# Block 0 of a convolution and feed-forward kernel: fp32 operands in its first layer replaced by three passes of 12-bit parts, with the order of the start rewritten

## The chip, the cores and the metric

The kernel runs on one core of one Trainium2 chip. The metric is the device time of one execution in microseconds (us): the median of several runs. The engines are TensorE (PE: matmuls; PEld is its weight load), VectorE (DVE), ScalarE (ACT), GpSimd (POOL) and SyncE (SP, which here only issues DMAs).

## The reference

`x` is 8 x 4096 x 192 in fp32, `weight` 8 x 7, `w_in` 192 x 2048 and `w_out` 2048 x 192. The two large weights are given in 64-bit floating point.

```python
w = exp(weight - max(weight)); w = w / (sum(w) + 1e-9)   # per head, 7 taps
out = einsum('hk,bskhg->bshg', w, windows(x))            # causal convolution along the sequence, 24 channels a head
x = out.reshape(32768, 192)
h = x @ w_in
g = h * clip(h + 3, 0, 6) / 6
result = (g @ w_out).astype(float32)
```

## The kernel before

**Blocks.** The 32768 tokens are 32 blocks of 1024 (two halves of 512, one half in the lower 64 partitions, one in the upper). Of each block, `y` (the convolution; three thirds of 64 channels per half) is multiplied by `w_in` (first layer: 8 chunks `c` of 128 columns and two groups, OWN with `y` as it lies, OTHER with the halves' partitions swapped by DMA), the gate is applied on ACT (`relu`, L308) and DVE (`gate`, L312), and `g` is multiplied by `w_out` (second layer).

**Blocks 1 to 31** write each operand of the first layer as parts of 12 significant bits. The high part is x times 1 - 2^-13, rounded to the short format fp32r as it is written; the low part is x minus the high one. `PASSES` then takes three products for each fp32 one: high by high, low weights by high y, full weights by low y. A unit of `first_layer` (L508) is 3 passes x 3 thirds x 2 halves = 18 matmuls into two banks of PSUM (a slot), then one relu and one gate over both banks. `second_layer` (L593) is a Strassen scheme in fp32.

**Block 0** works in plain fp32. `half_mm` (L302) does one third of one half; a part `(c, group)` is 6 matmuls into two banks, taken from a list of eight, with two relus and two gates of 512. `out_direct` (L347) is its second layer, in fp32: three groups of 64 matmuls; a group goes through the eight chunks of `w_out` in order, eight matmuls a chunk.

**The start, by engine order.** Everything from `tc.manual_schedule()` on runs on each engine in the order of the code. While block 0 begins, 16 units of weights (8 of `w_in`, then 8 of `w_out`, 384 columns each) are rounded from 64 to 32 bits by the class `Rounding`:

- `load`: DMA from SP into a stage buffer; unit n + 4 is loaded at the join of unit n.
- `split` (L177, L181): two bit operations on DVE, `scale` and `top`.
- `clamp` (L189, L192, L195): three operations on ACT.
- `join` (L198, L202 on DVE, then the product L206 on POOL), which writes the weights.

`stg` has 8 stage buffers, `cnv` 4 sets of work tiles. Of the convolution of block 0, third 2 is made on PE (seven taps as diagonal matrices, L794), third 0 on DVE in half-width taps (L261), third 1 on ACT (tap 0), DVE (taps 1 to 4) and PE (taps 5, 6). `begin` starts parts with the thirds 2 and 0 while third 1 is under way. The loop over the 16 parts joins, clamps and splits a unit in ten of its turns (`slots`); units 13 to 15 follow behind the loop. `prepare`, inside `out_direct`, then cuts all of `w_in` into its three parts with `w_parts` (ACT L480 and L487, POOL L483), convolves block 1 (L899) and cuts its y.

Since the start is laid out by hand, the time depends on which engine stands where when a unit's weights, a third of y or a slot is due.

Of the kernel before, what the change touches and what calls it, by code (L numbers as in the profile page):

```python
# [8 lines left out]
ALU = mybir.AluOpType  # L9
# [22 lines left out]
def kernel(  # L32
# [39 lines left out]
    start_pools, first_in = ExitStack(), ExitStack()  # L72
    stg = start_pools.enter_context(tc.tile_pool(name="stg", bufs=8))
    cnv = start_pools.enter_context(tc.tile_pool(name="cnv", bufs=4))
    fi = first_in.enter_context(tc.tile_pool(name="fi", bufs=1, side="right"))
# [40 lines left out]
    zeros = cnv.tile([P, N], F32, name="zeros", bufs=1)  # L116
    nc.vector.memset(zeros[:], 0.0)


    w_in = fi.tile([P, NP, K3, P], F32, name="w_in")  # L120


# [10 lines left out]
    def stage():  # L133
        return stg.tile([P, WS, 2], U32, name="stage")

    def load_w_in(j):
        st = stage()
        for half in range(2):
            nc.sync.dma_start(  # L139
                out=st[half * D2 : (half + 1) * D2].rearrange("p (s f) w -> p s (f w)", s=K3),  # L140
                in_=w_in_bits[j + half * NP].rearrange("p s f w -> p s (f w)"),
            )
        return st

    def load_w_out(j):
        st = stage()
        nc.sync.dma_start(
            out=st[:].rearrange("p (k d) w -> p k (d w)", k=2), in_=w_out_bits[:, j]
        )
        return st  # L150
# [7 lines left out]
    class Rounding:  # L158
# [13 lines left out]
        def split(self):  # L172
# [4 lines left out]
            nc.vector.tensor_scalar(  # L177
# [3 lines left out]
            nc.vector.tensor_scalar(  # L181
# [15 lines left out]
        def join(self):  # L197
# [9 lines left out]
                out=self.dst, in0=self.sig[:], in1=self.scale[:].bitcast(F32), op=ALU.mult  # L207
            )
    def w_in_unit(j):
        return Rounding(lambda: load_w_in(j), w_in[:, j].rearrange("p s f -> p (s f)"))  # L210

    def w_out_unit(j):
        dst = w_out[:, j, B11 : B22 + 1].rearrange("p b d -> p (b d)")
        return Rounding(lambda: load_w_out(j), dst)
# [29 lines left out]
    y_swapped = fi.tile([P, K3, N], F32, name="y_swapped")  # L244
    OWN, OTHER = 0, K3
# [29 lines left out]
    def swap_first(part):  # L275
        swap(y_swapped[:, part], y[:, part])

    g = cst.tile([P, NP, 2, G, N], F32, name="g")
# [6 lines left out]
    free_banks = list(range(2 * 4))  # L285

    def take():
        return free_banks.pop(0)

    def give(b):  # L290
        free_banks.append(b)

    def half_mm(k, b, w, third_of_y, start=False, stop=False, onto=False):

        r = slice(k * D2, (k + 1) * D2)  # L300
        src = y[r, third_of_y] if third_of_y < K3 else y_swapped[r, third_of_y - K3]
        nc.tensor.matmul(  # L302
            out=psum[:, b], lhsT=w[r], rhs=src, start=start, stop=stop,
            skip_group_check=onto,
        )
# [9 lines left out]

    def h_mm(c, group, bs, s, order=range(K3)):

        for k in range(2):
            half_mm(k, bs[k], w_in[:, c, s], group + s, s == order[0], s == order[-1])

    def g_of(c, group, k):

        return g[:, c, k, k if group == OWN else 1 - k]

    def h_out(c, group, bs, between):
        for k, b in enumerate(bs):
            relu(g_of(c, group, k), psum[:, b])
        between()
        for k, b in enumerate(bs):
            gate(g_of(c, group, k), psum[:, b])  # L330
            give(b)

# [44 lines left out]
    def out_direct(i, work):  # L383

        parts = [(k, q) for k in range(G) for q in range(G * NQ)]
        for r in range(0, len(parts), 4):
            b = take()
# [16 lines left out]
            give(b)  # L404
# [20 lines left out]

    def product(bank, j, n, q, ks=every, **tokens):
        x, w = prod[n]
        return mm(bank, j, S3 if n == 7 else x, w, q, ks, True, True, **tokens)

    def four(*parts):  # L430

        b = take()
        bank = psum[:, b]
        side_by_side(*[product(bank, j, n, q) for j, (n, q) in enumerate(parts)])
        return b, bank

    def three(n, n4, q4):
        return four(*[(n, q) for q in range(NQ)], (n4, q4))

    def by_quarters(n, q):  # L440

        b = take()
        bank = psum[:, b]
        w = NP // 4
        side_by_side(
            *[product(bank, j, n, q, range(j * w, (j + 1) * w)) for j in range(4)]
        )
        return b, bank
# [27 lines left out]
    def r32(ap):  # L476
        return ap.bitcast(F32R)

# [6 lines left out]
    def w_parts(high, low, full, w):  # L485
        high_of(high, w)
        nc.scalar.copy(out=r32(full), in_=w)  # L487
        low_of(low, w, high, nc.gpsimd)

    free_slots = list(range(4))  # L490
    y_own, y_other, pools, s1 = [], [None], [], []

    def swap_parts():
        y_other[0] = pools[0].tile([P, 2, K3, N], F32, name="y_other", tag="other")
        for n in range(2):
            swap(y_other[0][:, n], y_own[n])


    def first_layer(i, jobs):

        def unit(n):
            group, c = divmod(n, NP)
            slot = free_slots.pop(0)
            for m_, (wn, yn) in enumerate(PASSES):
                for s in range(K3):
                    for k in range(2):
                        r = slice(k * D2, (k + 1) * D2)
                        nc.tensor.matmul(  # L508
                            out=psum[:, 2 * slot + k], lhsT=r32(w_in_parts[wn][r, c, s]),
                            rhs=r32(y_other[0][r, yn, s] if group else y_own[yn][r, s]),  # L510
                            start=m_ == s == 0, stop=m_ == 2 and s == K3 - 1,
                            skip_group_check=True,
                        )
            both = psum[:, 2 * slot : 2 * slot + 2]
            to = g4[:, c, 1:3] if group else g4[:, c, 0::3]
            relu(to, both)
            gate(to, both)
            free_slots.append(slot)
# [259 lines left out]

    with tc.manual_schedule():
# [10 lines left out]
        pe_taps = KC - 2  # L790
# [8 lines left out]
        b = take()  # L799
        for _ in range(3):  # L800

            nc.tensor.matmul(
                out=psum[:, b], lhsT=zeros[:, 0:P], rhs=zeros[:], start=True, stop=True
            )
        for k in range(KC):
# [3 lines left out]
        b1 = take()  # L809
        pe_tap(b1, 1, pe_taps, pe_taps)  # L810


        order = (pe_third, 0, 1)
        parts = [(c, group) for p in range(0, NP, 2) for group in (OWN, OTHER)
                 for c in (p, p + 1)]
        early = {}

        def begin(c, group):
            early[c, group] = take(), take()
            for s in order[:2]:  # L820
                h_mm(c, group, early[c, group], s, order)
# [3 lines left out]
        for k, u in enumerate(conv0[: per + 2 * pe_taps]):  # L825
            if k == 5:
                split(0)
                clamp(0)
            elif k == per - 3:
                join(0, more=False)  # L830
                split(1)
                nc.scalar.copy(out=y[:, pe_third], in_=psum[:, b])
                give(b)
                swap_first(thirds[pe_third])
                clamp(1)
            elif k in (per, per + 1):
                if k == per:
                    swap_first(thirds[0])
                    load(AHEAD)
                    begin(0, OWN)  # L840
                    pe_tap(b1, 1, pe_taps + 1, pe_taps)
                continue
            elif k == per + 4:
                join(1)
                split(2)
                clamp(2)
            u()
        add(y[:, 1], psum[:, b1], y[:, 1])
        give(b1)
        swap_first(thirds[1])  # L850
        join(2)
        split(3)
        clamp(3)
        split(4)

        for c, group in ((0, OTHER), (1, OWN), (1, OTHER)):
            begin(c, group)
        for c, group in parts[: len(early)]:
            h_mm(c, group, early[c, group], order[2], order)

        slots = [0, 1, 3, 4, 6, 7, 9, 10, 12, 13]
        n = 3
        for slot, (c, group) in enumerate(parts):
            first = slot < len(early)
            if first:
                bs = early[c, group]
            else:
                bs = take(), take()
                for s in range(K3):
                    h_mm(c, group, bs, s)  # L870
            more = slot in slots

            def between():
                if more:
                    join(n)
                    clamp(n + 1)

            if slot == 6:
                x_tiles[1] = load_x(1)
            h_out(c, group, bs, (lambda: None) if first else between)  # L880
            if more:
                split(n + 2)
                if first:
                    between()
# [109 lines left out]
```

## Time and profile before

| | us |
|---|---|
| median of 3 runs (2225.63 to 2225.75) | 2225.64 |
| the profiled execution | 2225.73 |
| its span | 2223.6 |
| busy: PE, DVE, ACT, POOL | 2216.4, 1810.3, 938.1, 819.8 |
| chain that ended last: L593, L508, L302, L347 | 49%, 46%, 2%, 2% |
| relu 128x512 (L308), 128x1024 | 0.68, 1.12 |
| clamp L189, L192, L195 | 0.62, 0.62, 0.57 |
| product on POOL L206 on w_in, on w_out | 1.08, 1.04 |

Durations are the means of one instruction. On ACT and DVE the next instruction may start some 0.05 to 0.1 us before the end of the one ahead of it, so the distance between starts is the better price. The granted clock of PE was 0.999. A timeline row is: start, duration, engine, line, operation, output <- input, shape, and how many like ones are merged; in brackets stands the idle time before it and what ended it.

### The profile page before, as it was taken

The page shows a single profiled execution, that of the slowest core. Times are in us where ns is not written, and L with a number is a line of the kernel's source. Part 1 is how long each engine was busy: PE and PEld are TensorE (multiplying, and loading weights), DVE is VectorE, ACT ScalarE, POOL GpSimd, SP SyncE. Part 2 cuts the span into 40 slices and gives each one's busy share as a digit, 9 for nine tenths or more (in the row PEclk, how much of TensorE's full clock was granted, in tenths as well). Part 3 has the DMA queues.
Part 4 walks back from the last instruction along what each step waited for, and adds up shares of the span by engine and source line. Part 5 has one row for each costly group of instructions (what it writes and reads, how often), then busy time and mean ns, then how long its engine had stood idle before and what let it go on. Part 6 is the DMA issues. An engine that isn't in the chain of part 4 may idle for free.

```text
span 2223.6 us, 49133 instructions
## 1 busy us (share of the span) xinstructions
PE 2216.4 (100%) x21496; PEld 1536.0 (69%) x21496; DVE 1810.3 (81%) x1607; ACT 938.1 (42%) x1182; POOL 819.8 (37%) x692
## 2 busy tenths in 40 slices
PE   9999999999999999999999999999999999999999
PEld 5467776677766777766777667776677776677766
DVE  8788888887888888888888888888888888788866
ACT  7444443344433444334444334443344433344433
POOL 2434432344422444223443224442244432344322
PEclk9999999999999999999999999999999999999999
DMA  6233223333234342243322333323433224333232
GB/s 157 58 68 72 49 44 77 70 70 65 38 67 77 63 77 35 57 77 70 70 52 43 75 73 67 70 36 64 77 65 75 39 53 77 70 70 55 40 60 34
DMA packets 248613, 142.10 MB, mean 64 GB/s; under 512 B 207024, under 2 KB 212144, under 8 KB 248400
## 3 DMA queue, kind: packets, MB, share of 16 engines
q1 hardware_dynamic: 229912, 105.08, 23.3%
q0 software_dynamic: 17248, 33.64, 8.7%
q8 instruction: 168, 2.75, 0.5%
q10 hardware_dynamic: 1240, 0.27, 0.1%
q14 instruction: 45, 0.37, 0.1%
HBM read 31.72 MB, written 25.17 MB: 26 GB/s over the span
## 4 chain that ended last, share of the span: by engine, by line
PE 99%; DMA 0%; DVE 0%; SPq 0%; ACT 0%; issue 0%; DVEq 0%; ACTq 0%
PE psum L593 49%; PE psum L508 46%; PE psum L302 2%; PE psum L347 2%; DMA x<-in_x_dram 0%; SPq L106 0%; SPq L139 0%; DVE top L181 0%; PE psum L794 0%; DVE y L261 0%; DVE results L462 0%; SPq L95 0%; ACT y L808 0%; ACT scale L192 0%; ACT sig L195 0%
## 5 line engine op out<-in xcount | busy, mean ns | idle before, releaser
L593 PE MATMUL psum<-g,w_out 128*32 128x512 f32 (+1 forms) x6712 | 967.4, 552 | 0.0
L308 ACT ACTIVATE g<-psum,half 128x1024 f32<-128x1024 f32 (+1 forms) x528 | 574.2, 1092 | 487.8 <-PE psum L508 459.8
L312 DVE SCALAR_TENSOR_TENSOR g<-g,psum 128x1024 f32<-128x1024 f32 (+1 forms) x528 | 619.6, 1185 | 195.5 <-ACT g L308 195.1
L556 POOL TENSOR_TENSOR s<-g 128x256 f32<-128x256 f32 x248 | 267.0, 1077 | 1252.9 <-DVE g L312 877.3
L593 PEld LDWEIGHTS psum<-g,w_out 128*32 128x32 f32 x6712 | 371.8, 110 | 246.3 <-issue 126.9
L508 PE MATMUL psum<-y,w_in 64*128 64x512 f32 x4464 | 515.3, 388 | 0.0
L508 PE MATMUL psum<-y_other,w_in 64*128 64x512 f32 x4464 | 510.9, 386 | 0.0
L508 PEld LDWEIGHTS psum<-y,w_in 64*128 64x128 f32 x4464 | 415.8, 184 | 112.3 <-issue 26.0
L508 PEld LDWEIGHTS psum<-y_other,w_in 64*128 64x128 f32 x4464 | 418.1, 184 | 87.8
L593 PE MATMUL psum<-s,w_out 128*32 128x512 f32 (+1 forms) x3272 | 465.4, 570 | 0.0
L899 DVE SCALAR_TENSOR_TENSOR y<-x,c_sb,y 128x1536 f32<-128x1536 f32 x186 | 336.7, 1810 | 8.4 <-ACT y L897 7.2
L418 POOL TENSOR_TENSOR s<-g 128x1024 f32<-128x1024 f32 x93 | 297.8, 3203 | 25.0 <-DVE g L312 25.0
L593 PE MATMUL psum<-g,w_s 128*32 128x256 f32 x1240 | 282.8, 379 | 0.0
L593 PEld LDWEIGHTS psum<-s,w_out 128*32 128x32 f32 x3272 | 154.5, 110 | 80.2 <-issue 48.3
L593 PEld LDWEIGHTS psum<-g,w_s 128*32 128x32 f32 x1240 | 136.4, 110 | 67.7
L418 DVE TENSOR_TENSOR s<-g 128x2048 f32<-128x2048 f32 (+1 forms) x93 | 177.2, 1933 | 1.1
L593 PE MATMUL psum<-s,w_s 128*32 128x256 f32 x744 | 170.7, 379 | 0.0
L556 DVE TENSOR_TENSOR g<-g 128x1024 f32<-128x1024 f32 x124 | 151.7, 1224 | 6.0 <-DVE g L556 0.9
L418 DVE TENSOR_TENSOR g<-g 128x2048 f32<-128x2048 f32 x62 | 139.1, 2284 | 0.0
L462 DVE TENSOR_TENSOR p<-psum,p 32x256 f32<-32x256 f32 (+1 forms) x93 | 47.7, 513 | 95.5 <-PE psum L593 94.1
L462 DVE TENSOR_TENSOR results<-psum,results 32x256 f32<-32x256 f32 (+3 forms) x128 | 69.3, 541 | 51.1 <-issue 47.6
L590 ACT COPY psum<-psum 32x512 f32<-32x512 f32 x93 | 51.3, 551 | 135.3 <-PE psum L593 135.3
(87 smaller groups left out, 1152.4 us busy)
## 6 DMA issues: line engine op xcount, KB each, us to landing
y_other<-y SPq DMA_DIRECT2D x124, 384.0 KB, 5.0
g<-g POOLq DMA_DIRECT2D x62, 512.0 KB, 5.0
out_dram<-results SPq DMA_DIRECT2D x378, 64.0 KB, 2.0
x<-in_x_dram SPq DMA_DIRECT2D x53, 388.5 KB, 7.0
stage<-in_moe_w_in_dram SPq DMA_DIRECT2D x16, 192.0 KB, 4.6
stage<-in_moe_w_out_dram SPq DMA_DIRECT2D x8, 384.0 KB, 7.3
x<-in_x_dram SPq DMA_DIRECT2D x7, 384.0 KB, 6.5
x<-in_x_dram POOLq DMA_DIRECT2D x2, 388.5 KB, 5.4
```

Source lines behind the costliest of these rows:

```text
L302: nc.tensor.matmul(out=psum[:, b], lhsT=w[r], rhs=src, start=start, stop=stop, skip_group_check=onto,)
L308: nc.scalar.activation(r6, h, ACT.Relu, bias=half[:], scale=1.0 / 6.0)
L312: nc.vector.scalar_tensor_tensor(out=g_, in0=g_, scalar=1.0, in1=h, op0=ALU.min, op1=ALU.mult)
L347: lambda p=p: nc.tensor.matmul(out=bank[j * QS : (j + 1) * QS, tokens], lhsT=w_out[:, p, w, cols], rhs=x[:, p, tokens], start=(first and p ...
L418: engine.tensor_tensor(out=o[:, r], in0=a[:, r], in1=b[:, r], op=op)
L462: nc.vector.tensor_tensor(out=out, in0=x, in1=y, op=op)
L508: nc.tensor.matmul(out=psum[:, 2 * slot + k], lhsT=r32(w_in_parts[wn][r, c, s]), rhs=r32(y_other[0][r, yn, s] if group else y_own[yn][r, s ...
L556: engine.tensor_tensor(out=o, in0=p, in1=q, op=op)
L590: streams[3].append((t - 0.5, lambda: fn(*args, **kw)))
L593: nc.tensor.matmul(out=out, lhsT=w, rhs=x, start=start, stop=True, tile_position=(0, j * QS), skip_group_check=True,)
L899: jobs.append(lambda k=k: nc.vector.scalar_tensor_tensor(out=y[:], in0=x[:, :, k : k + N], scalar=c_sb[:, k : k + 1], in1=y[:], op0=ALU.mu ...
```

## The change

Everything concerns the start and block 0.

- The three parts of `w_in` are made unit by unit in a new step `part`: the high part on ACT, the full one as a copy and the low one as a subtraction on POOL, from `sig`, into which the product now goes. `part(n)` stands half a step behind `join(n)`: with the second of two units of the first layer. `w_parts` leaves `prepare`.
- The first layer of block 0 uses the three passes (`products`), slots of two banks, and one relu and one gate of 1024 a unit. The thirds of y are cut into high (ACT) and low (DVE) one by one, and both are swapped: twelve swap DMAs instead of six.
- Taps 3 to 6 of third 1 are on PE instead of taps 5 and 6.
- A unit of weights is joined with every second unit of the first layer, so eight in the loop (units 2 to 9) and six behind it (10 to 15).
- The stages of `w_in` lie in the part of `g` that is written last; `stg` has 4 buffers (for `w_out` alone) and `cnv` 3.

```diff
+    g = cst.tile([P, NP, 2, G, N], F32, name="g")
+    zeros = g[:, 0, 0, 0]
+    w_in_parts = [cst.tile([P, NP, K3, P], F32, name=f"w_in{n}") for n in range(3)]
+    y_own = [cst.tile([P, K3, N], F32, name=f"y{n}") for n in range(2)]
+    y_other = cst.tile([P, 2, K3, N], F32, name="y_other")
...
+    early_stages = [
+        g[:, c].rearrange("p h k n -> p (h k n)").bitcast(U32)[:, t : t + 2 * WS]
+        .rearrange("p (f w) -> p f w", w=2)
+        for c in range(NP - 4, NP) for t in (0, 2 * WS)
+    ]
...
             nc.gpsimd.tensor_tensor(
-                out=self.dst, in0=self.sig[:], in1=self.scale[:].bitcast(F32), op=ALU.mult
-            )
+                out=self.sig[:] if len(self.dst) > 1 else self.dst[0],
+                in0=self.sig[:], in1=self.scale[:].bitcast(F32), op=ALU.mult,
+            )
+
+        def part(self):
+            if len(self.dst) > 1:
+                high, low, full = self.dst
+                nc.scalar.mul(r32(high), self.sig[:], CUT)
+                nc.gpsimd.tensor_copy(out=r32(full), in_=self.sig[:])
+                nc.gpsimd.tensor_tensor(
+                    out=r32(low), in0=self.sig[:], in1=high, op=ALU.subtract
+                )
...
+    def products(n, slot, s, steps=range(3), begin=False, end=False):
+        group, c = divmod(n, NP)
+        for m_ in steps:
+            wn, yn = PASSES[m_]
+            for k in range(2):
+                r = slice(k * D2, (k + 1) * D2)
+                nc.tensor.matmul(
+                    out=psum[:, 2 * slot + k], lhsT=r32(w_in_parts[wn][r, c, s]),
+                    rhs=r32(y_other[r, yn, s] if group else y_own[yn][r, s]),
+                    start=begin and m_ == 0, stop=end and m_ == 2, skip_group_check=True,
+                )
...
-        pe_taps = KC - 2
+        pe_taps = 3
...
+        for u in conv0[5 : per - 3]:
+            u()
+        join(0, more=False)
+        split(1)
+        high_y(pe_third, psum[:, b : b + 1])
+        part(0)
+        clamp(1)
+        for u in conv0[per - 3 : per]:
+            u()
+        low_y(pe_third, psum[:, b : b + 1])
+        high_y(0, all_of(0))
+        low_y(0, all_of(0))
+        load(AHEAD)
+        thirds_of(0, (pe_third, 0))
+        join(1)
+        split(2)
+        for u in conv0[per + 2 : per + 2 * pe_taps]:
+            u()
+        part(1)
         add(y[:, 1], psum[:, b1], y[:, 1])
-        give(b1)
-        swap_first(thirds[1])
-        join(2)
+        high_y(1, all_of(1))
+        low_y(1, all_of(1))
+        clamp(2)
         split(3)
-        clamp(3)
-        split(4)
...
+        thirds_of(1, (pe_third, 0))
+        thirds_of(0, (1,), True)
+        thirds_of(NP, (pe_third, 0))
+        thirds_of(1, (1,), True)
+        thirds_of(NP, (1,), True)
...
+        n = 2
+        for at, k in enumerate([0, 1, NP, NP + 1] + [
+            c + group * NP for c in range(2, NP) for group in range(2)
+        ]):
...
+            relu(to, both)
+            if at % 2:
+                part(n)
+                clamp(n + 1)
+            else:
+                join(n)
+            gate(to, both)
+            free_slots.append(slot)
+            if at % 2:
                 split(n + 2)
-                if first:
-                    between()
                 n += 1
...
         def prepare():
-            for n in range(0, NP, 4):
-                r = slice(n, n + 4)
-                w_parts(*[w[:, r] for w in w_in_parts], w_in[:, r])
             for job in conv_jobs(1):
                 job()
```

`high_y` and `low_y` cut one third of y; `low_y` also issues its swaps. `thirds_of` begins or continues a unit with the thirds named. Of the units, n = c is OWN and n = NP + c is OTHER, with NP = 8.

More of the change, by code (lines that the diff above doesn't have):

```diff
@@ L71 @@
     ps = ctx.enter_context(tc.tile_pool(name="ps", bufs=1, space=bass.MemoryType.PSUM))
[L72 to L75, printed above, removed]
+    start_pools = ExitStack()
+    stg = start_pools.enter_context(tc.tile_pool(name="stg", bufs=4))
+    cnv = start_pools.enter_context(tc.tile_pool(name="cnv", bufs=3))
     def x_source(i):
@@ L115 @@
     diag = cnv.tile([P, KC, P], F32, name="diag", bufs=1)
-    zeros = cnv.tile([P, N], F32, name="zeros", bufs=1)
-    nc.vector.memset(zeros[:], 0.0)
-    w_in = fi.tile([P, NP, K3, P], F32, name="w_in")
+    g = cst.tile([P, NP, 2, G, N], F32, name="g")
+    zeros = g[:, 0, 0, 0]
+    nc.vector.memset(zeros, 0.0)
+    w_in_parts = [cst.tile([P, NP, K3, P], F32, name=f"w_in{n}") for n in range(3)]
+    y_own = [cst.tile([P, K3, N], F32, name=f"y{n}") for n in range(2)]
+    y_other = cst.tile([P, 2, K3, N], F32, name="y_other")
     w_out = cst.tile([P, NP, 7, DH], F32, name="w_out")
@@ L131 @@
     assert 2 * D == WS
-    def stage():
-        return stg.tile([P, WS, 2], U32, name="stage")
+    early_stages = [
[3 more added lines that the diff above has]
+    ]
     def load_w_in(j):
-        st = stage()
+        st = early_stages[j]
         for half in range(2):
@@ L145, in load_w_out @@
     def load_w_out(j):
-        st = stage()
+        st = stg.tile([P, WS, 2], U32, name="stage")
         nc.sync.dma_start(
@@ L149, in load_w_out @@
         )
-        return st
+        return st[:]
     EXP1 = 1 << 20
@@ L170, in load, with split @@
             self.st = self.load_words()
-        def split(self):
+        def split(self, engine=nc.vector):
             high = self.st[:, :, 1]
@@ L176, in split @@
             self.sig = cnv.tile([P, WS], F32, name="sig")
-            nc.vector.tensor_scalar(
+            engine.tensor_scalar(
                 out=self.scale[:], in0=high, scalar1=0x7FF00000, scalar2=None,
@@ L180, in split @@
             )
-            nc.vector.tensor_scalar(
+            engine.tensor_scalar(
                 out=self.top[:], in0=high, scalar1=0xFFFFF, scalar2=0x100000,
@@ L206, in join, with r32 @@
             nc.gpsimd.tensor_tensor(
-                out=self.dst, in0=self.sig[:], in1=self.scale[:].bitcast(F32), op=ALU.mult
-            )
+                out=self.sig[:] if len(self.dst) > 1 else self.dst[0],
+                in0=self.sig[:], in1=self.scale[:].bitcast(F32), op=ALU.mult,
+            )
+        def part(self):
[6 more added lines that the diff above has]
+                )
+    def r32(ap):
+        return ap.bitcast(F32R)
     def w_in_unit(j):
-        return Rounding(lambda: load_w_in(j), w_in[:, j].rearrange("p s f -> p (s f)"))
+        dst = [w[:, j].rearrange("p s f -> p (s f)") for w in w_in_parts]
+        return Rounding(lambda: load_w_in(j), dst)
     def w_out_unit(j):
         dst = w_out[:, j, B11 : B22 + 1].rearrange("p b d -> p (b d)")
-        return Rounding(lambda: load_w_out(j), dst)
+        return Rounding(lambda: load_w_out(j), [dst])
     def w_sums(sums):
@@ L243 @@
     y = ys.tile([P, K3, N], F32, name="y")
-    y_swapped = fi.tile([P, K3, N], F32, name="y_swapped")
-    OWN, OTHER = 0, K3
+    OWN, OTHER = range(2)
     def conv_units(i, parts, cuts=1):
@@ L273, in swap @@
         nc.sync.dma_start(out=to[0:D2], in_=part[D2:P])
-    def swap_first(part):
-        swap(y_swapped[:, part], y[:, part])
-    g = cst.tile([P, NP, 2, G, N], F32, name="g")
     g4 = g[:].rearrange("p c h k n -> p c (h k) n")
@@ L284 @@
     psum = ps.tile([P, 2 * 4, N], F32, name="psum")
[L285 to L304, printed above, removed]
-        )
+    free_slots = list(range(4))
     def relu(r6, h):
@@ L314, in gate @@
         )
[L316 to L327, printed above, removed]
-        between()
-        for k, b in enumerate(bs):
-            gate(g_of(c, group, k), psum[:, b])
-            give(b)
     def dff_half(k):
@@ L386, in out_direct @@
         for r in range(0, len(parts), 4):
-            b = take()
+            b = 2 * free_slots[r // 4]
             bank = psum[:, b]
@@ L403, in out_direct @@
             nc.vector.transpose(out=xt[:], in_=bank)
-            give(b)
             for j, (k, q) in enumerate(parts[r : r + 4]):
@@ L424 @@
     }
[L426 to L448, printed above, removed]
     def rows(q):
@@ L472 @@
     m = slice(0, DH)
-    def r32(ap):
-        return ap.bitcast(F32R)
     def high_of(out, x):
@@ L483, in low_of, with swap_parts, places @@
         engine.tensor_tensor(out=r32(out), in0=x, in1=high, op=ALU.subtract)
[L485 to L494, printed above, removed]
-        for n in range(2):
-            swap(y_other[0][:, n], y_own[n])
+    s1 = []
+    def swap_parts(thirds=slice(0, K3)):
+        for n in range(2):
+            swap(y_other[:, n, thirds], y_own[n][:, thirds])
+    def products(n, slot, s, steps=range(3), begin=False, end=False):
[9 more added lines that the diff above has]
+                )
+    def places(n, slot):
+        group, c = divmod(n, NP)
+        return g4[:, c, 1:3] if group else g4[:, c, 0::3], psum[:, 2 * slot : 2 * slot + 2]
     def first_layer(i, jobs):
         def unit(n):
-            group, c = divmod(n, NP)
             slot = free_slots.pop(0)
-            for m_, (wn, yn) in enumerate(PASSES):
+            for m_ in range(3):
                 for s in range(K3):
[L506 to L515, printed above, removed]
+                    products(n, slot, s, (m_,), s == 0, s == K3 - 1)
+            to, both = places(n, slot)
             relu(to, both)
@@ L777, in join, with part @@
             load(n + AHEAD)
+    def part(n):
+        units[n].part()
     with tc.manual_schedule():
@@ L797, in pe_tap @@
             )
-        b = take()
+        b, b1 = (2 * free_slots[-1] + k for k in range(2))
         for _ in range(3):
             nc.tensor.matmul(
-                out=psum[:, b], lhsT=zeros[:, 0:P], rhs=zeros[:], start=True, stop=True
+                out=psum[:, b], lhsT=zeros[:, 0:P], rhs=zeros, start=True, stop=True
             )
@@ L808 @@
         nc.scalar.mul(y[:, 1], x0[:, 1, 0:N], c_sb[:, 0:1])
[L809 to L815, printed above, removed]
-        early = {}
[L818 to L821, printed above, removed]
+        for k in range(pe_taps, KC):
+            pe_tap(b1, 1, k, pe_taps)
@@ new lines, with thirds_of, high_y, low_y @@
+        early = {}
+        def thirds_of(n, which, end=False):
+            if n not in early:
+                early[n] = free_slots.pop(0)
+            for s in which:
+                products(n, early[n], s, begin=s == pe_third, end=end)
+        def high_y(s, of):
+            high_of(y_own[HIGH][:, thirds[s]], of)
+        def low_y(s, of):
+            low_of(y_own[LOW][:, thirds[s]], of, y_own[HIGH][:, thirds[s]], nc.vector)
+            swap_parts(thirds[s])
+        def all_of(s):
+            return y[:, thirds[s]]
@@ L823 @@
         conv0 = conv_units(0, thirds[:pe_third], 2)
         per = len(conv0) // pe_third
[L825 to L846, printed above, removed]
-            u()
+        for u in conv0[:5]:
+            u()
@@ new lines @@
+        split(0)
+        clamp(0)
+        for u in conv0[5 : per - 3]:
[16 more added lines that the diff above has]
+            u()
@@ L848 @@
+        part(1)
         add(y[:, 1], psum[:, b1], y[:, 1])
-        give(b1)
-        swap_first(thirds[1])
-        join(2)
+        high_y(1, all_of(1))
+        low_y(1, all_of(1))
+        clamp(2)
         split(3)
-        clamp(3)
-        split(4)
[L856 to L861, printed above, removed]
@@ L862 @@
-        n = 3
-        for slot, (c, group) in enumerate(parts):
-            first = slot < len(early)
-            if first:
-                bs = early[c, group]
-            else:
[L868 to L881, printed above, removed]
+        thirds_of(1, (pe_third, 0))
@@ new lines @@
+        thirds_of(0, (1,), True)
[6 more added lines that the diff above has]
+        ]):
+            if at == 6:
+                x_tiles[1] = load_x(1)
+            if k in early:
+                slot = early[k]
+            else:
+                slot = free_slots.pop(0)
+                for m_ in range(3):
+                    for s in range(K3):
+                        products(k, slot, s, (m_,), s == 0, s == K3 - 1)
+            to, both = places(k, slot)
+            relu(to, both)
[7 more added lines that the diff above has]
+            if at % 2:
@@ L882 @@
                 split(n + 2)
-                if first:
-                    between()
                 n += 1
@@ L891 @@
         start_pools.close()
-        late = ctx.enter_context(tc.tile_pool(name="late", bufs=1, reuse_waits="tile"))
-        w_in_parts = [late.tile([P, NP, K3, P], F32, name=f"w_in{n}") for n in range(3)]
         def conv_jobs(i):
@@ L915, in prepare @@
         def prepare():
-            for n in range(0, NP, 4):
-                r = slice(n, n + 4)
-                w_parts(*[w[:, r] for w in w_in_parts], w_in[:, r])
             for job in conv_jobs(1):
                 job()
-            first_in.close()
-            later = ctx.enter_context(tc.tile_pool(name="later", bufs=1, reuse_waits="tile"))
-            y_own.extend(later.tile([P, K3, N], F32, name=f"y{n}") for n in range(2))
-            pools.append(ctx.enter_context(tc.tile_pool(name="oth", bufs=1, reuse_waits="tile")))
             x_tiles[2] = load_x(2, nc.gpsimd)
```

## The prediction

> **What bounds the kernel now.** The page says PE 100% busy, which says little, so I first read the chain of waits in order of time.
>
> ```profile
> 17.28 41.27 PE psum L302 x184
> 58.56 41.34 PE psum L347 x384
> 99.89 32.87 PE psum L508 x288
> ```
>
> Block 0's first layer (L302), its second (L347) and block 1's first layer (L508) follow each other without a gap. From 99.89 us on, 31 equal blocks of 32.87 + 35.47 us follow, which the change leaves alone: its worth is the shift of 99.89. L302 and L508 do the same work: 48 and 144 pairs of half products, 41.27 us for 46 pairs (0.90 each) against 32.87 (0.228 each). Operands of 12 bits are the cheaper: 16 units of 9 x 0.228 = 2.05 us, where 16 units now take 16 x 3 x 0.86 = 41.3. If PE were all, 8.4 us would go.
>
> Next the busy times in stretches of 10 us (columns: stretch, sum, PE, PEld, DVE, ACT, POOL, clock, DMA share, GB/s):
>
> ```profile
> 24.00:34.00 10.00, 10.00 (x47) 6.02 (x46) 8.82 (x20) 9.81 (x18) 2.01 (x2) 1.00 1.02 266
> 34.00:44.00 10.00, 10.00 (x47) 6.73 (x45) 10.00 (x20) 9.81 (x19) 4.19 (x4) 1.00 0.70 208
> 44.00:54.00 10.00, 10.00 (x48) 6.70 (x46) 9.71 (x22) 9.84 (x19) 2.17 (x4) 1.00 0.00 0
> ```
>
> ACT and DVE are as full as PE. ACT's timeline shows that it has no air in it:
>
> ```profile
> 42.19 0.61 ACT L189 ACTIVATE sig<-scale,bias_e 128x384 f32<-128x384 uint32 x1
> 42.84 0.61 ACT L192 ACTIVATE scale<-sig,bias_e 128x384 uint32<-128x384 f32 x1
> 43.48 0.57 ACT L195 ACTIVATE sig<-stage 128x384 f32<-128x384 uint32 x1
> 43.97 2.39 ACT L308 ACTIVATE g<-psum,half 128x512 f32<-128x512 f32 x4
> 46.24 0.61 ACT L189 ACTIVATE sig<-scale,bias_e 128x384 f32<-128x384 uint32 x1
> ```
>
> One clamp takes 1.78 us (42.19 to 43.97; the last of its three only 0.49), four relus 2.27 (0.57 each). Block 0 has 16 clamps and 32 relus. The last look is at DVE and POOL behind the layer:
>
> ```profile
> 60.95 0.55 DVE L198 SCALAR_TENSOR_TENSOR scale<-stage,scale 128x384 uint32<-128x384 uint32 x1
> ...
> 61.89 0.35 DVE L177 TENSOR_SCALAR scale<-stage 128x384 uint32<-128x384 uint32 x1
> 62.04 1.06 POOL L206 TENSOR_TENSOR w_out<-sig,scale 128x384 f32<-128x384 f32 x1 [4.46 <-DVE sig L202]
> 62.16 1.16 DVE L181 TENSOR_SCALAR top<-stage 128x384 uint32<-128x384 uint32 x1
> ...
> 63.24 0.55 DVE L198 SCALAR_TENSOR_TENSOR scale<-stage,scale 128x384 uint32<-128x384 uint32 x1
> ...
> 66.09 1.01 POOL L206 TENSOR_TENSOR w_out<-sig,scale 128x384 f32<-128x384 f32 x1 [0.50 <-DVE sig L202]
> ```
>
> L181 takes 0.35 elsewhere; started during POOL's product it takes 1.16 and ends with it. So a unit with a split goes round in 2.29 us (60.95 to 63.24), and from the join of unit 13 (60.95) to the end of the product of unit 15 (67.10) it is 6.15. The eight L347 matmuls on unit 15 (its chunk is the last of eight in group 0) begin 7 x 1.72 us after 58.56, at 70.6 (1.72 = 8 x 41.34 / 192). Unit 15 has 3.5 us to spare. That is the number the change uses up.
>
> **The change, step by step.** My sum is a time for unit 15's product, since only that chunk lets PE go on.
>
> *Until clamp 2.* Up to 12.7 us nothing moves. Then POOL has three operations a w_in unit instead of one. The copy has no row: one input of 128 elements took 0.29 (AFFINE_SELECT), two inputs 0.46 where DVE leaves it alone (L565) and 1.0 at 384 elements, so I scale 0.29 by 1.0 / 0.46 to 0.63; the ends are 0.29 and 1.08 (the mean of L206 on w_in). The subtraction is put at 1.0, as L206 of that shape. By the L181 row DVE's taps (0.41 each) and POOL's operations exclude each other, so I let them alternate. Top of unit 1 ends at 13.86; three taps, a copy and a subtraction 16.4; low of third 2 (0.65) and of third 0 (0.6) 17.7; join 1 (0.95) 18.65; split 2 (0.55) 19.2; POOL's product until 19.95; four taps, copy and subtraction 23.05; the sum with PE's taps (0.6) 23.65; the high part of third 1 on ACT (0.6) 24.25; clamp 2 behind it, 26.0. Without any exclusion it is 23.8. In this time ACT stands at two new waits with clamp 2 queued behind them: the high part of unit 1's weights waits for POOL's product (19.95), that of third 1 for the sum (23.65). Before, ACT had done clamp 3 as well by 24.2. The two taps more on PE (2 x 0.86) end at 15.75, ahead of what unit 0 waits for (17.5), and cost nothing; the two taps less on DVE (4 x 0.41 = 1.6 us) are in the sum.
>
> *Pairs 0 and 1.* Relu 0 runs 26.0 to 27.1. A 128x1024 relu is put at 1.07: 1.118 alone, less the 0.05 by which neighbours overlap above. Unit 1 is through on PE at 27.25 (low of third 1 at 24.9, unit 0's end 25.2, two thirds of unit NP 26.6, then 0.65), relu 1 to 28.4, the high part of unit 2's weights (0.46, as L195's pace; 0.59 if as the 512 copy) and clamp 3: pair 1 starts at 30.6. Its swapped third 1 lands at 29.0 to 29.5 (four DMAs of 0.58 from SP after 24.3, and 2.4 to landing by the y_swapped row; twice the swaps there were). Behind them on SP stand the loads of units 6, 7 and 8 to 11 and of x, issued from 27 to 34 us; unit 6 is split at 39. Clamp 4 ends at 35.1.
>
> *Pairs 2 to 7.* ACT needs 2.14 + 0.46 + 1.78 = 4.38, with handovers 4.45; PE 4.11 and is ahead. DVE and POOL go round join (1.09), product, copy, subtraction, split: 1.09 + 1.0 + 0.63 + 1.0 + 0.6 = 4.3. So ACT: 35.1 + 4 x 4.45 = 52.9; pair 6 has no weights' high part, 3.95: 56.85; two relus 59.0; clamp 10, 60.8.
>
> *The tail.* Before, three units were joined behind the layer, now six (two parts share one unit). Join 10 at 60.85, three turns of 2.29 to join 13 at 67.7, and 6.15 more: 73.85. Then 1.72 + 2 x 13.78 for the other groups: **103.1 against 99.89, +3.3 us.** The stages' four buffers make the load of units 12 to 15 wait for the join four units earlier, at 52.9, 56.9, 60.8 and 63.1. The trace's w_out load with DMA idle (issued 39.91) lands in 3.6 us, so unit 14's words are there at 64.4, its split is at 66.3: hidden. With the 7.3 us of the page's median, taken while the stages filled side by side, it would be 1.8 us late.
>
> *Behind it.* The weights' parts leave the prepare step (four ACT operations of 1.47 us, 6.9 us of POOL). They were hidden: y's low part ended at 88.2, needed at 99.89, and by the same row the conv then starts near 73 instead of 73.9. Worth nothing. Blocks 1 to 31 are the same.
>
> The profiled execution took 2225.73 us (span 2223.6 and 2.1 around it; the median is 2225.64): 2225.73 + 3.3 = **2229.0**.
>
> **A row and a rule.** The trace has PE slow once: the six L802 records at the start took 4.99 us (0.83 each), the sixteen L794 records of the same shape 7.07 (0.44). Afterwards PE never waited longer than 1.1 us, so no row shows whether a wait brings this back. In my schedule PE waits from 18.4 (end of unit 0's two thirds) to 22.3 (unit 1's low weights) but for one pair of 0.23 us. The Trainium skill, "TensorE: Matmul & The Clock Gate", Part 1, says that the array falls to half its clock after an idle window of about 3.4 us and needs as long a busy stretch to recover; it counts against this change, and gives rival B.
>
> **Rivals.**
> A, slower: POOL's copy costs as much as its product. At 1.08 the round of DVE and POOL is 4.77 and takes ACT's place: 4 x 0.32 + 2 x 0.45 in the start, +2.2, so 2231.2. It passes 0.2% (4.45 us, 1.15 over the forecast) from a copy of 0.91 us: 1.15 = 2 x (c - 0.63) + 4 x (c - 0.76), 0.76 being where the round reaches ACT's 4.45. For it: POOL's two-input rows are slow; against: the one-input row.
> B, slower: PE resumes at 22.3 at the rate of the L802 row, 1.9 times as slow. Unit 1's thirds still end before unit 0 is waited for, but two thirds of NP and one of unit 1 take 3.9 us instead of 2.05 and unit 0's last third 0.4 more: relu 1 starts at 29.6 instead of 27.3, and all of ACT follows: 3.3 + 2.3 = +5.6, 2231.3. For it: this wait is three times the longest in the trace. Against it: it isn't empty, and relu 1 alone has to bear it.
> C, not slower: the rounding of w_out never holds PE. Then the layer ends at 31.75 + 12 x 2.054 = 56.4, and 41.34 later it is 97.7: -2.2, 2223.5. Against: ACT's own sum, 17.1 + 2.8 + 23.1 = 43 us behind 26.0.
> D, faster: the start does not wait either; 15.75 + 32.87 + 41.34 = 90.0: -9.9, 2215.8. The same sum forbids it.
>
> **How the numbers follow.** The forecast has 0.60; without exclusion in the start it is 2227, with the upper price of the high part 2229.5, inside 0.2%. A 0.18, B 0.13, C 0.06, D 0.03. 0.2% is 4.45 us, about what a measurement of this kernel can tell from no change. Faster is D, 0.03; the same is the forecast and C, 0.66; slower is A and B, 0.31. The range reaches from C, 2223.5, to A or B with the other half of their cause, 2233.
>
> **What would show it.** ACT without gaps from about 31 us; two relus, a high part and a clamp every 4.4 to 4.5 us; six joins of 2.29 us behind the layer; PE waiting on w_out in group 0 of L347's successor, and block 1 starting at 103. Wrong if that start comes before 98 (ACT does not bind), if POOL's copy is over 0.9, or if PE's pairs take 0.45 us anywhere after 22.

## The result and the profile after

The changed kernel takes **2230.01 us** (median of 16 runs, 2228.81 to 2230.86) where the kernel before takes 2225.68 us in the same comparison (2225.60 to 2225.84): a ratio of 1.0019, 95% interval 1.0011 to 1.0027, or +4.33 us. The forecast was +3.3 us, 2229.0. The change is slower, and the interval leaves out 1, though the loss is slightly less than 0.2%. The profiled execution took 2230.25 us, with a span of 2228.5. Line numbers below are those of the changed kernel: L439 is its first layer, L317 `out_direct`, L302 the relu, L306 the gate, L210 POOL's product, L202 and L206 the join.

The chain of waits of the changed kernel (start, duration, what) shows how block 0 ends:

```profile
68.67 3.57 POOL w_out L210 x2
...
72.73 2.51 POOL w_out L210
...
75.29 29.39 PE psum L317 x272
104.68 1.35 PE psum L439 x9
```

Block 1 starts at 104.68 us instead of 99.89. Ahead of it stand, without a gap, the last eight matmuls of group 0 and two whole groups, and ahead of those the product of unit 15 on POOL. That is the chain the forecast named; it put the product's end at 73.85, and it was 75.23.

PE in the same stretch shows one wait after another, each ended by a unit of `w_out` (the brackets hold the idle time and what ended it):

```profile
55.91 1.92 PE L317 MATMUL psum<-g,w_out 128*32 128x512 f32 x16
58.88 1.92 PE L317 MATMUL psum<-g,w_out 128*32 128x512 f32 x16 [1.05 <-POOL w_out L210]
62.72 1.92 PE L317 MATMUL psum<-g,w_out 128*32 128x512 f32 x16 [1.92 <-POOL w_out L210]
66.24 3.64 PE L317 MATMUL psum<-g,w_out 128*32 128x512 f32 x32 [1.59 <-POOL w_out L210]
71.00 3.64 PE L317 MATMUL psum<-g,w_out 128*32 128x512 f32 x32 [1.12 <-POOL w_out L210]
75.29 4.93 PE L317 MATMUL psum<-g,w_out 128*32 128x512 f32 x44 [0.65 <-POOL w_out L210]
```

So the first layer did get shorter: PE leaves it at 55.9 instead of 58.5. From 55.9, the 41.34 us of the second layer would have ended at 97.3; block 1 starts 7.4 us later than that. The five waits in brackets add up to 6.3 us; the rest is that a burst of 16 matmuls between two waits takes 1.92 us instead of its share of 1.72.

The busy times in stretches show what the forecast had only as a rival, a drop of the granted clock (column PEclk, after POOL):

```profile
18.00:19.00 1.00, 0.23 (x4) 0.00 (x0) 1.00 (x3) 0.00 (x0) 0.58 (x1) 1.00 0.94 205
19.00:20.00 1.00, 0.00 (x0) 0.00 (x0) 1.00 (x2) 0.51 (x1) 0.94 (x2) 1.00 0.93 209
20.00:21.00 1.00, 0.50 (x2) 0.19 (x2) 1.00 (x2) 0.01 (x1) 0.94 (x2) 0.98 0.93 203
21.00:22.00 1.00, 0.77 (x4) 0.68 (x6) 1.00 (x3) 0.00 (x0) 0.17 (x1) 0.50 0.70 162
...
27.00:28.00 1.00, 1.00 (x8) 0.78 (x6) 0.82 (x1) 0.00 (x0) 0.65 (x2) 0.60 0.74 157
28.00:29.00 1.00, 1.00 (x12) 0.82 (x10) 0.00 (x0) 0.31 (x1) 0.00 (x0) 1.00 0.99 293
```

PE does next to nothing from 18.2 to 21.2 us and then has half its clock until about 27.6. ACT's relus show what this costs and how the layer then runs:

```profile
25.45 1.12 ACT L302 ACTIVATE g<-psum,half 128x1024 f32<-128x1024 f32 x1
28.69 1.12 ACT L302 ACTIVATE g<-psum,half 128x1024 f32<-128x1024 f32 x1 [2.12 <-PE psum L439]
...
36.05 2.12 ACT L302 ACTIVATE g<-psum,half 128x1024 f32<-128x1024 f32 x2
...
40.25 2.11 ACT L302 ACTIVATE g<-psum,half 128x1024 f32<-128x1024 f32 x2
```

Relu 1 comes at 28.69, forecast 27.3. The pairs then follow every 4.2 us, as against 4.45. Last, DVE, ACT and POOL at the end of the tail:

```profile
70.91 1.33 POOL L210 TENSOR_TENSOR w_out<-sig,scale 128x384 f32<-128x384 f32 x1
70.93 1.57 ACT L845 ACTIVATE y<-x,c_sb 128x1536 f32<-128x1536 f32 x1
...
71.28 1.37 DVE L206 SCALAR_TENSOR_TENSOR sig<-top,sig 128x384 f32<-128x384 uint32 x1
72.58 4.27 DVE L847 SCALAR_TENSOR_TENSOR y<-x,c_sb,y 128x1536 f32<-128x1536 f32 x2
72.73 2.50 POOL L210 TENSOR_TENSOR w_out<-sig,scale 128x384 f32<-128x384 f32 x1 [0.49 <-DVE sig L206]
```

Unit 15's product takes 2.50 us where 1.0 is usual. DVE had begun the convolution of block 1 (L847, 1.8 us a tap) 0.15 us earlier. The forecast puts the start of unit 15's product at 72.84 (73.85 less 1.01); it started at 72.73, but ran against this tap.

### The profile page after: what moved, and what is told of

It is laid out like the page before. It is cut to its first block, busy times and chain, and to the rows that moved or that the text cites. A ratio compares the mean times of both kernels' runs of the same rounds, so it can differ in the third digit from the quotient of the medians.

```text
span 2228.5 us, 49336 instructions
## 1 busy us (share of the span) xinstructions
PE 2212.9 (99%) x21596; PEld 1537.8 (69%) x21596; DVE 1811.0 (81%) x1590; ACT 935.1 (42%) x1172; POOL 832.5 (37%) x706
## 4 chain that ended last, share of the span: by engine, by line
PE 97%; ACT 1%; DVE 1%; POOL 0%; issue 0%; DMA 0%; DVEq 0%; ACTq 0%; SPq 0%; POOLq 0%
PE psum L535 49%; PE psum L439 46%; PE psum L317 1%; ACT g L302 1%; PE psum L739 0%; POOL w_out L210 0%; PE psum L747 0%; ACT scale L196 0%; DVE g L306 0%; ACT sig L199 0%; ACT sig L193 0%; DMA stage<-in_moe_w_out_dram 0%; ACT w_in L218 0%; DVE scale L202 0%; DVE sig L206 0%
## 5 line engine op out<-in xcount | busy, mean ns | idle before, releaser
L302 ACT ACTIVATE g<-psum,half 128x1024 f32<-128x1024 f32 x512 | 571.6, 1118 | 495.4 <-PE psum L439 467.3
L306 DVE SCALAR_TENSOR_TENSOR g<-g,psum 128x1024 f32<-128x1024 f32 x512 | 618.3, 1218 | 198.1 <-ACT g L302 197.8
L439 PE MATMUL psum<-y,w_in 64*128 64x512 f32 x4608 | 535.8, 389 | 2.5 <-ACT w_in L218 1.8
L439 PE MATMUL psum<-y_other,w_in 64*128 64x512 f32 x4608 | 529.8, 387 | 0.0
L439 PEld LDWEIGHTS psum<-y,w_in 64*128 64x128 f32 x4608 | 430.1, 185 | 120.3 <-issue 26.0
L439 PEld LDWEIGHTS psum<-y_other,w_in 64*128 64x128 f32 x4608 | 432.7, 184 | 90.7
L847 DVE SCALAR_TENSOR_TENSOR y<-x,c_sb,y 128x1536 f32<-128x1536 f32 x186 | 335.7, 1805 | 1.2
```

The lines of the kernel that those rows point to most:

```text
L302: nc.scalar.activation(r6, h, ACT.Relu, bias=half[:], scale=1.0 / 6.0)
L306: nc.vector.scalar_tensor_tensor(out=g_, in0=g_, scalar=1.0, in1=h, op0=ALU.min, op1=ALU.mult)
L439: nc.tensor.matmul(out=psum[:, 2 * slot + k], lhsT=r32(w_in_parts[wn][r, c, s]), rhs=r32(y_other[r, yn, s] if group else y_own[yn][r, s]), ...
L847: jobs.append(lambda k=k: nc.vector.scalar_tensor_tensor(out=y[:], in0=x[:, :, k : k + N], scalar=c_sb[:, k : k + 1], in1=y[:], op0=ALU.mu ...
```

## The experiments

The theory after these readings: block 0 ends when the rounding of `w_out` ends, not when PE could; in that chain are (1) ACT's work in the layer, (2) the start, by DVE's chain and by PE's clock, (3) DVE and POOL keeping each other out in the tail, the convolution's first tap included.

**Unit 15's product alone on DVE.**

```diff
-            nc.gpsimd.tensor_tensor(
+            engine.tensor_tensor(
...
-        units[n].join()
+        units[n].join(nc.vector if n >= 15 else nc.gpsimd)
```

> The product of unit 15 alone moves from POOL to DVE, behind its join. Theory (the convolution of block 1, which starts at 72.58 us on DVE, kept POOL's product out until 74.2): the product ends near 73.2 instead of 75.23, block 1 starts at 102.6 instead of 104.68, the time falls by 2.0 us to 2228.0. Rival (the convolution costs nothing; unit 15 is late by the rounding chain alone): the product only becomes the 0.5 us shorter that DVE is than POOL, block 1 starts at 104.2.

Measured: 2228.77 us (ratio to the kernel before 1.0015, 1.0006 to 1.0023), 1.2 us below the changed kernel; block 1 starts at 103.07. Unit 15's product and PE's last wait in this execution:

```profile
71.93 0.56 DVE L210 TENSOR_TENSOR w_out<-sig,scale 128x384 f32<-128x384 f32 x1
```

```profile
70.25 32.82 PE L317 MATMUL psum<-g,w_out 128*32 128x512 f32 x304 [1.11 <-POOL w_out L210]
```

The product takes 0.56 and ends at 72.5; out of the tap's way it is no longer the last thing that PE waits for. But the gain is 1.2 and not 2.0. The reason is what is late next: PE goes on at 70.25, released by unit 13, and needs until 73.7 for chunks 5 and 6, so that chunk 7 no longer waits. With unit 13 as the last wait, the trace of the changed kernel would give a start of block 1 at 71.00 + 32.82 = 103.8, 0.9 us earlier. That block 1 starts even at 103.07 here is in part a better start: join 10 stands at 59.79 instead of 60.52. The runs of the two kernels overlap (2227.85 to 2230.10 here), so the times alone do not exclude the rival's 0.5 us; the next experiment shows the cause without moving the product.

**The convolution delayed by added work on ACT.**

```diff
         def prepare():
+            for n in (0, 4, 0, 4):
+                full = w_in_parts[FULL][:, n : n + 4]
+                nc.scalar.copy(out=r32(full), in_=full)
             for job in conv_jobs(1):
```

> Four ACT copies of 128x1536 (1.46 us each; the full part of w_in onto itself, no value changes) are put back where the weights' parts stood before, ahead of the convolution of block 1. Theory: the convolution starts near 78.4 instead of 72.58, the product of unit 15 runs its undisturbed 1.0 us and ends near 73.8, block 1 starts at 103.2, 1.5 us earlier although work is added. Rival (the removed step is worth nothing either way): block 1 starts at 104.7 as in the changed kernel, or later.

Measured: 2229.08 us (1.0014, 1.0005 to 1.0023), 0.9 us faster although 5.9 us of ACT work were added. The profile of this run, POOL's last two products:

```profile
69.11 1.26 POOL L210 TENSOR_TENSOR w_out<-sig,scale 128x384 f32<-128x384 f32 x1 [1.24 <-DVE sig L206]
70.87 1.01 POOL L210 TENSOR_TENSOR w_out<-sig,scale 128x384 f32<-128x384 f32 x1 [0.49 <-DVE sig L206]
```

The product of unit 15 is back at 1.01: the step that `prepare` lost had been holding the convolution off POOL. What that costs is less sure. The runs overlap with those of the changed kernel (2227.30 to 2230.10 here), and the profiled execution, 2227.30 us, is the fastest of its 11. The clock stayed at 1.00 in it, and block 1 starts at 101.46 (this and the other starts read from a PE timeline lie 0.07 us before those of the chain, as 104.68). Beside the next experiment but one, which has no drop either (102.88), that is 1.4 us. Of these, some 0.6 belong to a tail that happened to go in regular turns here: in the other execution PE still waited for unit 13 until 69.27, so that without the tap block 1 would have started there at about 102.1.

**The second layer of block 0 chunk by chunk across its three groups.**

```diff
-        for r in range(0, len(parts), 4):     # a group: all eight chunks, then the next group
...
+        for p in every:                       # a chunk: all three groups, then the next chunk
+            for bank, group in zip(banks, groups):
...
```

The diff is shortened, and the two comments are added here. The three banks are those of the first two slots, and the list of slots is turned by two behind it, so that block 1 begins on other banks.

> The second layer of block 0 takes chunk 0 of all three groups, then chunk 1 of all three, so a unit of w_out is due every 5.17 us instead of every 1.72, the last one at 92 us. Theory (only the rounding of w_out sets the end of block 0): PE goes on from 55.9 without a wait, block 1 starts at 55.9 + 41.34 = 97.3 to 97.5, the time falls by 7.2 us to 2222.8, below the kernel before. Rival (PE or the start of block 1 is held elsewhere: y of block 1, transposes, slots): less than half of that.

Measured: **2222.74 us** (0.9987, 0.9978 to 0.9996), 7.3 us below the changed kernel and 2.9 below the kernel before. PE in this run:

```profile
56.54 41.41 PE L317 MATMUL psum<-g,w_out 128*32 128x512 f32 x384
97.88 12.31 PE L439 MATMUL psum<-y,w_in 64*128 64x512 f32 x106
```

No wait is left, and unit 15 (POOL's last products run from 71.38 to 75.6) is ready long before it is due. Behind the first layer nothing else holds PE in block 0; the first layer itself still ends only at 56.5.

**Products of zeros on PE in the wait at 18 us.**

```diff
         thirds_of(0, (pe_third, 0))
+        for _ in range(3):
+            nc.tensor.matmul(
+                out=psum[:, b], lhsT=zeros[:, 0:P], rhs=zeros, start=True, stop=True
+            )
         join(1)
```

> Three fp32 products of zeros (0.86 us each) stand on PE between unit 0's two thirds and unit 1, where PE waited from 18.2 to 20.07. Theory (the granted clock of 0.50 from 21 to 27.5 us came from that wait and made relu 1 start at 28.69): the clock stays at 1.00, relu 1 starts near 27.4, everything on ACT and block 1 come 1.0 to 1.3 us earlier, 103.4 to 103.7. Rival (relu 1 is held by something else, or the swapped third of y at 28.5 us holds PE anyway): clock 1.00, but block 1 within 0.3 us of 104.68.

Measured: 2228.66 us (1.0013, 1.0004 to 1.0022), 1.35 below the changed kernel, and the runs lie within 0.37 us of each other (2228.46 to 2228.83) where those of the changed kernel spread over 2.05. The clock is 1.00 in every stretch, and relu 1 comes earlier:

```profile
14.00:24.00 10.00, 8.83 (x38) 4.10 (x38) 9.17 (x15) 3.92 (x8) 3.83 (x5) 1.00 0.68 162
24.00:34.00 10.00, 9.53 (x80) 6.89 (x78) 8.69 (x15) 9.15 (x15) 5.09 (x6) 1.00 1.02 229
```

```profile
27.03 1.12 ACT L302 ACTIVATE g<-psum,half 128x1024 f32<-128x1024 f32 x1 [0.65 <-PE psum L439]
```

Block 1 starts at 102.88. Relu 1 was held by the clock: the 16 runs of the changed kernel have a mean granted clock of 0.997 to 0.999, the 11 of this version 0.999 or 1.000. The clock differs from run to run: the execution with the delayed convolution had no drop without any product of zeros, and its relu 1 came at 27.11.

**More ACT work in the layer.**

```diff
                 part(n)
+                nc.scalar.copy(out=diag[:, 0:3], in_=diag[:, 3:6])
                 clamp(n + 1)
```

> Each of the eight pairs of units in block 0's first layer gets one more ACT operation ahead of its clamp, a copy of 128x384 between tiles that nothing reads any more (0.41 us from start to start). Theory (ACT sets the pace there, 4.18 us a pair against 4.11 of PE): every pair takes 0.4 us longer and block 1 starts 8 x 0.41 = 3.3 us later, 2233.3. Rival (PE sets the pace and ACT has room behind it): under 1 us.

Measured: 2232.09 us (1.0030, 1.0018 to 1.0041), 2.1 above the changed kernel. The pairs grew as forecast, by 0.4 us, to 4.6 us each:

```profile
35.37 2.11 ACT L302 ACTIVATE g<-psum,half 128x1024 f32<-128x1024 f32 x2
39.95 2.12 ACT L302 ACTIVATE g<-psum,half 128x1024 f32<-128x1024 f32 x2
44.56 2.10 ACT L302 ACTIVATE g<-psum,half 128x1024 f32<-128x1024 f32 x2
```

ACT sets the pace of the layer. The 3.3 us do not all arrive. In this execution, the fastest of its six, block 1 starts only 1.1 us later, at 105.80: the start had the full clock for longer, and relu 1 came at 27.21 instead of 28.69. (PE's clock fell again behind a wait of 2.6 us in the tail, 0.83 over 64 to 74, but PE waited for unit 15 afterwards all the same.) What took the rest in the timed runs, 2.1 us by the median, stays open.

**Two taps back on DVE.**

```diff
-        pe_taps = 3
+        pe_taps = KC - 2
```

> Taps 3 and 4 of third 1 go back from PE to DVE, as in the kernel before. Theory (DVE's chain to third 1's sum sets clamp 2 and so the start of the layer): four half taps of 0.41 us more, clamp 2, relu 0 and block 1 1.6 us later, 2231.6. Rival (PE is as late, by the clock and the swapped third): less than 0.5 us.

Measured: 2232.03 us (1.0028, 1.0018 to 1.0039), 2.0 above the changed kernel. Relu 0 starts at 27.00 instead of 25.45, the 1.6 us of the four half taps, and PE's wait grows with it (a clock of 0.71 over 14 to 24 us). Which part of the 2.0 us is the taps and which the clock is not separated. The move of the taps to PE is a part of the change that gains.

**The products of units 10 to 15 on DVE.** The edit is that of the first experiment, from n = 10 on.

> The products of units 10 to 15 move from POOL to DVE. Theory (the two engines keep each other out in the tail): a unit takes 0.95 + 0.46 + 0.54 = 1.95 us on DVE without a wait, unit 15 is done at 71.2 instead of 75.23, block 1 starts at 100.5 instead of 104.68, 2225.8. Rival (ACT's clamps or the loads of the stages set the tail): unit 15 not before 73.

Measured: 2226.88 us (1.0005, 0.9997 to 1.0014), 3.1 below the changed kernel. On DVE two units in a row:

```profile
66.11 0.56 DVE L202 SCALAR_TENSOR_TENSOR scale<-stage,scale 128x384 uint32<-128x384 uint32 x1
66.57 0.56 DVE L206 SCALAR_TENSOR_TENSOR sig<-top,sig 128x384 f32<-128x384 uint32 x1
67.16 0.56 DVE L210 TENSOR_TENSOR w_out<-sig,scale 128x384 f32<-128x384 f32 x1
...
68.18 0.56 DVE L202 SCALAR_TENSOR_TENSOR scale<-stage,scale 128x384 uint32<-128x384 uint32 x1
```

A unit takes 2.07 us (66.11 to 68.18; I had 1.95), unit 15 is done at 71.3, and block 1 starts at 100.96. Neither ACT nor the loads set the tail.

**Chunk order and products of zeros together.**

> The chunk order across the three groups and the three products of zeros together. Theory: the layer ends at 55.2 as with the zeros alone, then 41.34 without a wait, block 1 starts at 96.6, about 2221.4 and as little spread as with the zeros alone. Rival (the chunk order has taken up what the clock cost): 2222.7 as without the zeros.

Measured: 2222.49 us (0.9986, 0.9977 to 0.9995), runs from 2222.31 to 2222.79. Block 1 starts at 96.88, close to the 96.6 expected, but the gain over the chunk order alone is 0.25 in the median, not 1.3, and the two sets of runs overlap. Eight of the eleven runs of the chunk order alone were at 2222.4 to 2222.9, and only two, the profiled one among them, at 2223.6. The rival came nearer. Most of those runs have the same mean clock of 0.998 as the profiled one, so the clock fell in them too; why it cost them less stays open. This is the fastest version of the study, 3.2 us below the kernel before.

**Control: the chunk order in the kernel before.**

> Control: the kernel before with the chunk order across the three groups and nothing else. Theory (there PE never waited for w_out, unit 15 had 3.5 us to spare): no change, within 0.3 us of 2225.7. Rival (the chunk order is faster by itself, and the 12-bit operands gained nothing): as much below 2225.7 as the changed kernel with this order is, 3 us.

Measured: 2225.68 us against 2225.68 (1.0000, 0.9991 to 1.0009); block 1 starts at 99.83. The order alone is worth nothing there. The 3 us of the version above come from the change itself, the 12-bit first layer with its new start, once `w_out` no longer holds PE.

**The DVE tail and the products of zeros together, chunk order as in the change.**

> The changed kernel in its own chunk order with two edits together, the three products of zeros on PE and the products of units 10 to 15 on DVE. Theory (the clock and the mutual exclusion in the tail are separate terms): 1.2 us below the DVE tail alone, 2225.7, the time of the kernel before, and a spread under 0.5 us. Rival (each takes up the other's gain): 2226.9 as with the DVE tail alone.

Measured: 2225.80 us (1.0001, 0.9992 to 1.0010), runs from 2225.73 to 2225.95; block 1 starts at 99.91. The two gains nearly add up: 3.1 and 1.35 alone, 4.2 together. Together they take back nearly all of the +4.33 us.

## Why the prediction was right, point by point

- *Where the end is set.* Right: unit 15's product, with ACT, DVE and POOL ahead of it and 29.3 us of PE behind it. The chain shows it, and the chunk order, which takes the units of `w_out` off the path and changes nothing else, gives back 7.3 us.
- *Until clamp 2.* 26.0 was forecast, relu 0 started at 25.45 behind it. DVE's taps and POOL did exclude each other (three half taps took 2.31 us and four 2.65, where one alone takes 0.41), but less often than in strict turns. Strict turns of the terms named would even have given about 26.5: they add up to 2.86 and 3.27 us where the sum moves on by 2.54 and 3.10. The two taps on PE were rightly counted as a gain (experiment: 2.0 us, the clock's part included).
- *Pairs 0 and 1.* Here the step failed in size: pair 1 was to begin its relus at 30.6 and did at 31.86, pair 2 at 36.05 instead of 35.1, because PE had half its clock. This was rival B, with a chance of 0.13. It came true in part, with relu 1 at 28.69 between the forecast's 27.3 and B's 29.6: PE fell to half clock, but the wait was shorter than I had it (unit 1's low weights came at 21.2, not 22.3). Its price is 1.35 us by the median, not 2.3. The row from which B took the slow rate, L802, has 1.00 in the clock column; the rows from 21 us on are the ones that show half a clock.
- *Pairs 2 to 7.* 4.45 us forecast, 4.2 measured: two adjacent relus take 2.0 us and not 2.14, and no handover had to be added. ACT does set the pace (experiment: 0.4 us of work, 0.4 us a pair). Over six pairs this gave back 1.3 us, and join 10 began at 60.52, forecast 60.85: two misses that cancelled, which was luck.
- *POOL's copy.* 0.51 us, put at 0.63 with ends of 0.29 and 1.08. Rival A is out.
- *The tail.* Six units instead of three, as forecast. The turns were not regular in the profiled run (2.3, 1.5, 3.3, 1.5, 1.4), yet join 15 ended within 0.1 us of the forecast's. The products of units 11 and 13 were kept out as well, by the DVE operations of the next unit: 63.93 to PE's restart at 66.24, and 68.67 to 71.00, about 2.3 us each. In the executions with the delayed convolution, with the chunk order and with the two taps back, the turns were regular, 2.3 us as in the forecast, and those products took 1.05 to 1.07; from join 10 to the end of join 15 it was 11.9 us with the delayed convolution, 12.1 here. What decides between the two patterns stays open. DVE and POOL are the limit there, by the experiment with the products on DVE.
- *Behind it.* "Worth nothing" for the weights' parts that leave `prepare` was wrong. I had asked only whether the moved-up convolution is hidden, not what it excludes when it starts. It starts on DVE beside unit 15's product and stretches it from 1.0 to 2.5 us. This is the 1.4 us by which unit 15 missed the forecast; in time it is worth about 1 us (0.9 by the trace, 0.9 and 1.2 by the medians of the two experiments), since unit 13 is nearly as late. It is the term that the sum lacked.
- *Rivals C and D.* The sum of ACT behind clamp 2 was rightly held against both. C's time, 2223.5, is the one that the chunk order reaches (2222.7) by taking `w_out` out of the way.
- *The last sum.* 103.1 less 99.89 is 3.2, where +3.3 is written; nothing hangs on the 0.1.

## What to carry to other kernels

A cheaper matmul moves the end only as far as the next thing PE waits for: add up the other engines' work in that stage before the gain is counted, and look for an order of the consumers that makes the late operand due later; here this gave 7.3 us, where taking POOL's products over to DVE gave 3.1. When a step is taken off an engine, ask what starts earlier in its place and which operation on the path that will hold up.

## What the runs showed of the hardware

- The granted clock fell to 0.50 after 3.0 us (18.2 to 21.2) in which PE still worked for 0.5 us, its longest single wait being 1.83 us, and came back after about 6.5 us of nearly full work. With the delayed convolution PE stood still even for 2.07 us in the same place, and the clock stayed at 1.00. The Trainium skill, "TensorE: Matmul & The Clock Gate", Part 1, gives an idle window of about 3.4 us that runs freely. That the outcome varies agrees with a free-running window; that the clock fell without 3.4 us of idling does not, and here the measurement decides.
- A product on POOL that started 0.15 us after a DVE tap with two tensor inputs (L847, x and y, 1.8 us) took 2.50 us, against 1.01 for the same product with that tap out of the way. The difference, 1.49 us, is about what was left of the tap (an estimate from these rows: 1.65).
